# An S4 convolution beside multi-query attention: setup transfers, the order of the first arguments and keys, and SyncE in emission order

## The chip, the cores and the metric

The kernel runs on one core of a Trainium2 chip. The metric is the device time of one execution in microseconds (us). The engines are TensorE (PE), VectorE (DVE), ScalarE (ACT), GpSimd (POOL) and SyncE (SP, which only issues transfers).

## The reference

Two independent blocks on sequences of 2048 positions, their outputs side by side. All is float32.

```python
# block A: a diagonal state-space model, 576 channels, 128 states, as an FFT convolution
dt = exp(log_dt)[:, None]
logdA = dt * (A_re + 1j * A_im)
P = exp(logdA[:, :, None] * arange(2048))
K = einsum("dn,dnl,dn->dl", Cc, P, dt * Bc).real
y = irfft(rfft(pad(u)) * rfft(pad(K)))[:2048] + u * Dskip
# block B: attention with 32 heads of 18, one key and one value head for all
q = heads(x @ wq); k = x @ wk; v = x @ wv
p = softmax(einsum("bhqd,bkd->bhqk", q, k) * 18 ** -0.5)
b = merge(einsum("bhqk,bkd->bhqd", p, v)) @ wo
out = concatenate([y, b], axis=-1)
```

## The kernel before

The attention sets the pace. A main loop goes in steps of three exponentials: PE makes scores `s` (L493, 128 x 1024, in pairs of matmuls of `aug`, the queries, against `kaug`, the keys), ACT takes `P = exp(s)` (L502, L504), PE adds the products `ops` of `P` with the values (L802). There are 1024 such exponentials of 128 x 1024. The queries of a head are projected, split, and sent through DRAM (`qd`) into `aug` by loads on SP (L481, L482).

Between these, a planner puts the pieces of all other work: query and output projections and the convolution. It is run while the kernel is built. Each piece is a step of a generator (`Stream`), with a cost and a due time from a model of the engines (`Clock`); constants at the top (`RATE`, `PACE`, `LEAD`, `GAP` and more) say how early or late a piece may be taken. All this fill work writes one PSUM bank, so the next piece on PE waits until DVE has copied out the one before.

The convolution goes in 12 chunks of 48 channels. `front(k)` makes a chunk's kernel: `factors(k)` works out powers of the state matrix (`r`, `f`, `m`, `w`: arguments on DVE, exponentials and sines on ACT, then products on DVE), `tables` and `kgen` turn them into `kg` on PE, and DVE copies this into `ksb`. At the end, `ksb` is stored to DRAM as `kd` (L1187) and loaded again in another layout as `kt`, by four loads (L1189) that wait until `kd` has landed. `front(k + 1)` starts at once behind it, while `back(k)` transforms the inputs (`hu`, `lu` on PE, copied out to `scu` by DVE) and the kernel (`hk`, `lk`). Factors are made for two chunks at a time: an even chunk computes its own and those of the next, and stores the next chunk's as `park` in DRAM; the odd chunk loads them (`w`, `r`, `f`, `m`, L1075) and goes on with the products `r<-r,m` and `f<-f,m` on DVE.

The order of the instructions on PE, ACT and DVE is the order in which the program emits them. On SP (and POOL) a scheduler of the language sets it, by its own estimate of when each transfer can go.

In the setup, `x0`, `wq`, `wkv`, `xr` are loaded; PE projects the first queries (`qps`, `qc`, `rows`), then keys and values (`kps`, `kv`) of all 2048 positions, chunk by chunk of the 576 inputs (`project`). `kc` is a copy of the keys, `keys` their rounded form and its remainder, and `place_keys` sends both into `kaug`, the placed keys. `conv.begin(n)` lets the convolution emit its next steps at that point.

Of the kernel before, what the change touches and what calls it, by code (L numbers as in the profile page):

```python
# [9 lines left out]
F32 = mybir.dt.float32  # L10
F32R = mybir.dt.float32r
I32 = mybir.dt.int32
AF = mybir.ActivationFunctionType
# [4 lines left out]
P = 128  # L18
# [3 lines left out]
DH = 18  # L22
# [15 lines left out]
NP = 8  # L38


RATE = 3.7138
PACE = 3.4622
AHEAD = 0.5907
TOTAL = 375.4872
LAST = 732.5081
DEFER = 0.3214
NAUG = 5
LEFT = 2.4801
CAP = 1.4415
DEBT = 0.4509  # L50
GROUP = 0.1798
HOLD = 0.2063
LEAD = 1.4122
MOST = 0.6584
LEAST = 0.4776
NEAR = 0.65
SLOPE = 0.6122
SOON = 1.3784
URGENT = 9.2035
BACK = 2  # L60
HELD = 0
GAP = 0.2804
GAP_NEW = 0.4872

LATE = {1: [0], 3: [1], 5: [2], 6: [3]}

# [138 lines left out]
class Attention:  # L205
# [36 lines left out]
    def setup(self, tp, conv):  # L242
# [22 lines left out]
        self.x0 = x0 = self.xp.tile([P, 5, CT], F32, name="x0", tag="x")  # L265

        conv.early()
        for k in range(5):
            if k % 2 == 0:
                e = min(k + 2, 5)  # L270
                nc.sync.dma_start(self.wq[0][:, k:e, :], a["wq"][0, :, k:e, :])
            nc.sync.dma_start(x0[:, k, :], a["xT"][0, :, k, :] if k < 4 else a["xe"][0])
        nc.sync.dma_start(wkv, a["wkv"])
        nc.scalar.dma_start(place, a["place"])
        for k in range(4):
            nc.sync.dma_start(xr[:, k], a["xT"][1:4, :, k, :].rearrange("c p n -> p c n"))
            if k == 1:
                nc.sync.dma_start(xe, a["xe"][1])
        nc.scalar.dma_start(spread, a["spread"])
# [33 lines left out]
        conv.begin(9)  # L313
        nc.scalar.activation(qc[:mn, :], qps[:mn, :], AF.Copy)
        for j in range(2):
            matmul4(nc, rows[:, j, :], place[:mn, 1 + j, :], qc[:mn, :])
        for j in range(2):
            nc.scalar.activation(self.ring[j], rows[:, j, :], AF.Copy)
        conv.begin(1)
        ab = self.p2.tile([P, 3], F32, tag="ab", name="ab0_0")  # L320
        V.tensor_reduce(ab[:mn, 0:1], qc[:mn, :], axis=AX.X, op=ALU.max, apply_absolute_value=True)
        conv.begin(6)
        for j in range(2):
            put(self.ring[j], rows[:, j, :], 1 + j)
# [4 lines left out]
        nc.scalar.activation(self.kc, kps, AF.Copy)  # L329
        project(pv, 32, 3)  # L330
        matmul4(nc, kq[:, 1, :], place[:, 0, :], self.kc)
        V.tensor_reduce(km[:, 4:5], self.kc, axis=AX.X, op=ALU.max, apply_absolute_value=True)
        V.tensor_scalar(km[:, 0:4], spread[:, FLAG:FLAG + 4], km[:, 4:5], None, op0=ALU.mult)
        pk = self.bank(4, "kmx")
        nc.tensor.matmul(pk, spread[:, 0:P], km[:, 0:4], start=True, stop=True)
        nc.scalar.activation(keys[:, 0, :], self.kc, AF.Copy)
# [3 lines left out]
        put(self.kaug[:, 0:CT], kq[:, 1, :], 0)  # L340
        self.side_work = side = Stream(self.side(keys[:, 3, :], keys[:, 4, :], aw), self.k, 99.0)
        while self.queried == 0:
            side.advance()
        pk = self.ps_o.tile([P, CT], F32, tag="o", name="kmx4")[:, :16]
# [3 lines left out]
        nc.scalar.activation(self.vt, pv, AF.Copy)  # L348
        V.tensor_tensor(keys[:, 1, :], self.kc, keys[:, 0, :].bitcast(F32), op=ALU.subtract)
        for t, r in ((0, 0), (0, 36), (1, 18)):  # L350
            self.place_keys(keys[:, t, :], r)
# [13 lines left out]

    def values(self):
        nc, V, K = self.nc, self.V, self.k
        vp = self.bank(CT, "vp").rearrange("p (j n) -> p j n", j=4)
# [598 lines left out]
class Conv:  # L967
# [57 lines left out]
    def arguments(self, k, w, f, r, m):  # L1025

        nc, V, K = self.nc, self.V, self.k
        tt = V.tensor_tensor
        mu, ad, sb = ALU.mult, ALU.add, ALU.subtract
        raw = self.raw.pop(k)  # L1030
        dt = raw[:, 6, :]
        nc.scalar.activation(dt, dt, AF.Exp)
        yield "v", K.act(0.25) + 0.2, False
        tt(raw[:, 0:4, :], raw[:, 0:4, :], dt.unsqueeze(1).broadcast_to([P, 4, ND]), op=mu)
        av, bv, br, bi, cr, ci = (raw[:, j, :] for j in range(6))
        V.tensor_scalar(bv, bv, 1.0 / (2 * math.pi), None, op0=mu)
# [4 lines left out]
        tt(m, ch(av), row(1), op=mu)  # L1041
        yield "v", 0.0, False
        tt(w[:, 2, :], ci, bi, op=mu)
        tt(f, ch(bv), row(0), op=mu)
        if k < 2:
            nc.scalar.activation(m, m, AF.Exp)
        yield "v", 0.0, False
        tt(w[:, 1, :], cr, bi, op=mu)
        V.tensor_scalar(r, f, MAGIC, -MAGIC, op0=ad, op1=ad)
        yield "v", 0.0, False  # L1050
        tt(w[:, 0, :], w[:, 0, :], w[:, 2, :], op=sb)
        tt(f, f, r, op=sb)
        yield "v", 0.0, False
        tt(w[:, 2, :], ci, br, op=mu)
        V.tensor_scalar(r.bitcast(I32), f.bitcast(I32), 0x7FFFFFFF, None, op0=ALU.bitwise_and)
        yield "v", 0.0, False
        tt(w[:, 1, :], w[:, 1, :], w[:, 2, :], op=ad)
        if k > 1:
            self.load(k + 2)

    def factors(self, k):
# [10 lines left out]
        if k % 2:  # L1072
            n = ND * NF
            for j, t in enumerate((f, r, m, w)):
                nc.sync.dma_start(t, self.parked[:, j * n:min((j + 1) * n, 3 * n + 3 * ND)].rearrange("p (c n) -> p c n", n=t.shape[2]))  # L1075
            yield "v", K.t + 7.0, False
        else:
            two = p1.tile([P, 3 * ND * NF + 3 * ND], F32, tag="tab", name=f"two{k}")
            part = lambda j, n: two[:, j * ND * NF:j * ND * NF + n * ND].rearrange("p (c n) -> p c n", n=NF if n == NF else ND)
            f2, r2, m2, w2 = part(0, NF), part(1, NF), part(2, NF), part(3, 3)  # L1080
            yield from self.arguments(k, w, f, r, m)
            yield "v", 0.0, False
            yield from self.arguments(k + 1, w2, f2, r2, m2)
            yield "v", K.v + 0.3, False

            if k > 0:
                nc.scalar.activation(m, m, AF.Exp)
                nc.scalar.activation(m2, m2, AF.Exp)
            K.act(2.5)
            yield "b", K.v + 0.3, False  # L1090
            for a, b in ((r, f), (r2, f2)):
                nc.scalar.activation(a, a, AF.Sin, scale=-TWO_PI, bias=self.hp)
                nc.scalar.activation(b, b, AF.Sin, scale=TWO_PI)
            if k == 0:
                nc.scalar.activation(self.one, self.one, AF.Exp)
                for j in (2, 3):
                    self.load(j)
            self.parked = self.dr.tile([P, 3 * ND * NF + 3 * ND], F32, tag="park", name=f"park{k}")
            nc.sync.dma_start(self.parked, two)
            yield "v", K.act(7.7) + 0.3, False  # L1100
        tt(r, r, m, op=mu)
        yield "v", 0.0, False
        tt(f, f, m, op=mu)
# [208 lines left out]
    def early(self):  # L1312
        nc = self.nc
        nc.scalar.dma_start(self.con, self.a["con"])
        self.load(0, nc.scalar)
        self.load(1, nc.scalar)
        self.n = -1
        self.streams = [Stream(self.front(0), self.k)]

# [55 lines left out]
def build(tc, **aps):  # L1375
# [109 lines left out]
```

## Time and profile before

| | us |
|---|---|
| median of 3 runs | 1194.89 (1194.51 to 1195.13) |
| the profiled execution | 1192.97 |
| its span in the profile | 1191.2 |
| PE busy | 1137.7 |
| ACT busy | 1041.7 |
| DVE busy | 989.0 |
| POOL busy | 53.9 |
| first exponential of the loop starts at | 29.23 |

A row of the timeline has the start, the duration, the engine and its line, the operation with output and inputs, and in brackets the idle time of the engine ahead of it with what ended it. `SPq` and `POOLq` are the queues by which transfers are issued: their durations are those of issuing, not of the transfer. A row of the windows has the length, each engine's busy time, the clock granted to PE, the DMA engines' share and their GB/s. A row of the costliest groups has busy time and mean ns of one, then the engine's idle time ahead of them and what ended most of it.

### The profile page before, as it was taken

The numbers are of one execution on the slowest core, as the hardware profiler recorded it, in microseconds if no ns is written. First come the engines' busy times: TensorE is split into PE (matmuls) and PEld (weight loads), VectorE is DVE, ScalarE is ACT, GpSimd is POOL, SyncE is SP. The second block draws the span as 40 slices with busy tenths as digits, with TensorE's granted clock in tenths as the row PEclk, the third lists the DMA queues.
The fourth block names the chain that finished last, engine by engine and source line by source line (L and its number), as shares of the span: only waits on it lengthen the run. The fifth ranks groups of instructions, "written<-read, shape, count | busy, mean of one in ns | idle before, by whom it ended". The sixth has DMA issues, their size and how long they took to land.

```text
span 1191.2 us, 41260 instructions
## 1 busy us (share of the span) xinstructions
PE 1137.7 (96%) x17954; PEld 599.6 (50%) x17954; DVE 989.0 (83%) x1733; ACT 1041.7 (87%) x1095; POOL 53.9 (5%) x104
## 2 busy tenths in 40 slices
PE   8999999899999999999989999999999989999997
PEld 2455455455555455555535545544544545544543
DVE  6859969986996985996997798598799797799576
ACT  5889899989898988889888988999998998998993
POOL 1100100111000000010000000001000000000000
PEclk9899999999999999999989999999999999999999
DMA  8541232424123123122233401223401221410201
GB/s 296 174 148 52 97 128 62 150 90 170 58 84 106 66 90 130 59 99 91 72 124 116 143 28 36 88 71 111 138 31 55 98 114 53 148 47 21 76 29 57
DMA packets 50185, 113.34 MB, mean 95 GB/s; under 512 B 6964, under 2 KB 17300, under 8 KB 48719
## 3 DMA queue, kind: packets, MB, share of 16 engines
q1 hardware_dynamic: 43919, 95.88, 23.2%
q0 software_dynamic: 5360, 14.03, 3.3%
q8 instruction: 143, 2.34, 0.8%
q10 hardware_dynamic: 720, 0.73, 0.2%
q14 instruction: 43, 0.35, 0.1%
HBM read 61.51 MB, written 48.45 MB: 92 GB/s over the span
## 4 chain that ended last, share of the span: by engine, by line
PE 53%; DVE 36%; ACT 4%; DMA 3%; issue 3%; SPq 1%; DVEq 0%; ACTq 0%
PE ops L802 21%; PE s L493 15%; DVE tab L128 7%; DVE acc L128 5%; DVE ks L128 4%; PE op L202 3%; PE iy L202 3%; ACT P L504 3%; DVE pt L128 2%; PE kg L1168 2%; PE q L202 2%; DVE tt L128 2%; DVE two L128 1%; DVE sck L128 1%; PE lu L202 1%
## 5 line engine op out<-in xcount | busy, mean ns | idle before, releaser
L504 ACT ACTIVATE P<-s 128x1024 f32<-128x1024 f32 x992 | 943.4, 1032 | 111.3 <-PE s L493 102.3
L802 PE MATMUL ops<-P,v_sb 128*32 128x256 f32 x8192 | 540.0, 382 | 6.3 <-DVE o L132 6.1
L493 PE MATMUL s<-aug,kaug 55*128 55x512 f32 x2048 | 351.6, 439 | 8.3 <-ACT P L504 7.2
L802 PEld LDWEIGHTS ops<-P,v_sb 128*32 128x32 f32 x8192 | 242.3, 110 | 191.6 <-issue 58.3
L493 PEld LDWEIGHTS s<-aug,kaug 55*128 55x128 f32 x2048 | 167.5, 185 | 203.6 <-ACT P L504 108.3
L202 PE MATMUL op<-wo_sb,oT 126*32 126x288 f32 (+1 forms) x1144 | 84.1, 410 | 7.2 <-DVE ob L132 6.3
L202 PE MATMUL q<-x,wq_sb 128*32 128x256 f32 x1200 | 78.7, 392 | 4.5 <-DVE un L140 2.2
L132 DVE COPY ksb<-kg 128x192 f32<-128x192 f32 x48 | 17.3, 361 | 67.0 <-PE kg L1168 66.9
L128 DVE TENSOR_TENSOR tab<-tab,tt 128x576 f32<-128x576 f32 (+1 forms) x72 | 59.0, 820 | 1.3
L128 DVE TENSOR_TENSOR tab<-sum,r 128x576 f32<-128x576 f32 (+1 forms) x72 | 58.8, 816 | 0.0
L128 DVE TENSOR_TENSOR tab<-r,dif 128x576 f32<-128x576 f32 (+1 forms) x72 | 58.7, 815 | 0.0
L128 DVE TENSOR_TENSOR tab<-tab 128x576 f32<-128x576 f32 (+1 forms) x72 | 58.6, 814 | 0.0
L128 DVE TENSOR_TENSOR tt<-f,sum 128x576 f32<-128x576 f32 (+1 forms) x72 | 58.6, 814 | 0.0
L202 PEld LDWEIGHTS q<-x,wq_sb 128*32 128x32 f32 x1200 | 37.0, 112 | 37.7 <-issue 9.4
L128 DVE TENSOR_TENSOR acc<-acc,pt 128x864 f32<-128x864 f32 (+2 forms) x72 | 54.3, 754 | 1.4
L128 DVE TENSOR_TENSOR pt<-us,ks 128x864 f32<-128x864 f32 (+2 forms) x72 | 54.2, 753 | 1.3
L202 PEld LDWEIGHTS op<-wo_sb,oT 126*32 126x32 f32 (+1 forms) x1144 | 32.1, 109 | 44.6 <-issue 9.6
L128 DVE TENSOR_TENSOR u<-u,iy 128x384 f32<-128x384 f32 x24 | 13.3, 553 | 38.3 <-PE iy L202 38.1
L1168 PEld LDWEIGHTS kg<-tab 128*32 128x32 f32 x2304 | 37.1, 110 | 15.0 <-issue 5.8
L1168 PE MATMUL kg<-tab 128*32 128x64 f32 x2304 | 41.5, 220 | 3.0 <-DVE tab L128 2.5
L128 DVE TENSOR_TENSOR ks<-ks 128x576 f32<-128x576 f32 (+1 forms) x48 | 41.0, 853 | 0.7
L202 PE MATMUL iy<-w,dft_sb 128*32 128x192 f32 x768 | 37.6, 328 | 3.5 <-DVE ql L128 2.6
(160 smaller groups left out, 996.9 us busy)
## 6 DMA issues: line engine op xcount, KB each, us to landing
aug<-qd SPq DMA_DIRECT2D x124, 108.0 KB
park<-two SPq DMA_DIRECT2D x6, 1944.0 KB
od<-o SPq DMA_DIRECT2D x31, 256.0 KB
qd<-qh POOLq DMA_DIRECT2D x30, 256.0 KB, 2.9
u<-u SPq DMA_DIRECT2D x12, 480.0 KB
kd<-ksb SPq DMA_DIRECT2D x12, 384.0 KB
kt<-kd SPq DMA_DIRECT2D x48, 96.0 KB
outa<-u SPq DMA_DIRECT2D x12, 384.0 KB
```

The costliest lines, as they stand in the source:

```text
L128: return self.v.tensor_tensor(out, a, b, **k)
L132: return self.v.tensor_copy(out, src)
L202: nc.tensor.matmul(ps[j:e], w[:, j:e], x, start=start, stop=stop, tile_position=(0, j))
L493: nc.tensor.matmul(ps[:, j, :], self.kaug[r, kb * P:(kb + 1) * P], t[r, :], start=True, stop=True)
L504: nc.scalar.activation(pt, ps, AF.Exp, scale=SCALE)
L802: nc.tensor.matmul(o_ps[32 * j:32 * j + 32, cs], self.v[:, kb, :], pts[2 * n + j // 2][:, j % 2, cs], start=(kb + f == 0), stop=(kb + f == ...
L1168: nc.tensor.matmul(ps[32 * g:32 * g + 32, d, :], t[:, :32], t[:, 32:], start=(j == 0), stop=(j == 1), tile_position=(0, 32 * g))
```

## The change

- The first transfers: `wq` of the first query group in two pieces instead of three, `x0` in two pieces of two and one of one instead of five; `place` goes by SP instead of ACT, `spread` and the second `raw` by POOL.
- In the setup the first chunks' arguments are emitted in another order, and a chunk's sines as soon as its arguments are there; `put` of the first queries comes earlier.
- Keys are projected ahead of three of the five value projections; the copies `kc`, `keys` and `vt` are made by DVE instead of ACT; two value projections come later, one of them after the first scores.
- `place_keys` stores a part of the keys to DRAM (`kr`) and loads it into `kaug` with three transfers per part and queue pair, where 18 transfers went from SBUF to SBUF.
- SP is taken into the engines whose order is that of emission.
- All constants of the planner have new values.

```diff
-RATE = 3.7138
-PACE = 3.4622
+RATE = 6.5889
+PACE = 3.8504
...
-        for k in range(5):
-            if k % 2 == 0:
-                e = min(k + 2, 5)
-                nc.sync.dma_start(self.wq[0][:, k:e, :], a["wq"][0, :, k:e, :])
-            nc.sync.dma_start(x0[:, k, :], a["xT"][0, :, k, :] if k < 4 else a["xe"][0])
+        for k, e in ((0, 2), (2, 4)):
+            w = slice(k, e if k == 0 else 5)
+            nc.sync.dma_start(self.wq[0][:, w, :], a["wq"][0, :, w, :])
+            nc.sync.dma_start(x0[:, k:e, :], a["xT"][0, :, k:e, :])
+        nc.sync.dma_start(x0[:, 4, :], a["xe"][0])
         nc.sync.dma_start(wkv, a["wkv"])
-        nc.scalar.dma_start(place, a["place"])
+        nc.sync.dma_start(place, a["place"])
...
-        for k in (0, 1, 4, 2):
+        for k in (0, 1):
             project(kps, 0, k)
             project(pv, 32, k)
-        project(kps, 0, 3)
-        nc.scalar.activation(self.kc, kps, AF.Copy)
-        project(pv, 32, 3)
-        matmul4(nc, kq[:, 1, :], place[:, 0, :], self.kc)
+        for k in (4, 2, 3):
+            project(kps, 0, k)
+        project(pv, 32, 4)
+        V.tensor_copy(kc, kps)
+        matmul4(nc, kq[:, 1, :], place[:, 0, :], kc)
...
-    def place_keys(self, t, r):
-
-        for c in range(1, NCH):
-            for b in (0, 64):
-                (self.nc.sync if b else self.nc.gpsimd).dma_start(self.kaug[b + r:b + r + 18, c * CT:(c + 1) * CT].bitcast(F32), t[32 * c:32 * c + 18, :].bitcast(F32))
+    def place_keys(self, n, t, *rows):
+
+        kd = self.dr.tile([P, CT], F32, tag="kr", name=f"kr{n}", bufs=2)
+        self.nc.sync.dma_start(kd, t.bitcast(F32))
+        kd = kd.rearrange("(c d) n -> d c n", c=4)[:DH, 1:]
+        for r in rows:
+            for b, q in ((0, self.nc.sync), (64, self.nc.gpsimd)):
+                q.dma_start(self.kaug[b + r:b + r + DH, CT:].bitcast(F32).rearrange("d (c n) -> d c n", c=3), kd)
...
+            def sines(cos, sin):
+                nc.scalar.activation(sin, sin, AF.Sin, scale=TWO_PI)
+                nc.scalar.activation(cos, cos, AF.Sin, scale=-TWO_PI, bias=self.hp)
+            one, two_ = self.arguments(k, w, f, r, m), self.arguments(k + 1, w2, f2, r2, m2)
+            if k == 0:
+                take = lambda g, n: [next(g, None) for _ in range(n)]
+                take(one, 2)
+                take(two_, 1)
+                take(one, 1)
+                take(two_, 1)
+                yield "v", 0.0, False
+                take(one, 9)
+                sines(r, f)
+                yield "v", 0.0, False
...
-        with tc.manual_schedule(engines={mybir.EngineType.PE, mybir.EngineType.Activation, mybir.EngineType.DVE}):
+        with tc.manual_schedule(engines={mybir.EngineType.PE, mybir.EngineType.Activation, mybir.EngineType.DVE, mybir.EngineType.SP}):
```

Where the chunks 0 and 1 meet, SP's order was this (`od0` is the attention's output of a first pair of heads, `aug2` the next queries; the numbers behind the names tell tiles of one name apart):

```order
L513 DMA od0_362<-o0_0_955 128x512
L1075 DMA r1_1150<-park0_250 128x1248
L1075 DMA f1_1149<-park0_250 128x1248
L1075 DMA m1_1151<-park0_250 128x1248
L1187 DMA kd0_1140<-ksb0_511 128x768
L1189 DMA kt0_1139<-kd0_1140 32x4x192 x4
L481 DMA aug2_113<-qd0_309 54x1x512
L482 DMA aug2_113<-sd0_310 1x512
```

And now, at the same place on SP:

```order
L522 DMA od0_340<-o0_0_944 128x512
L1213 DMA kd0_1187<-ksb0_500 128x768
L1215 DMA kt0_1186<-kd0_1187 32x4x192 x4
L1084 DMA f1_1196<-park0_380 128x1248
L1084 DMA r1_1197<-park0_380 128x1248
L1084 DMA m1_1198<-park0_380 128x1248
L1084 DMA w1_1195<-park0_380 128x144
L490 DMA aug2_113<-qd0_296 54x1x512
```

The reloads of chunk 1's parked factors have moved from ahead of the store `kd` to behind the four loads `kt` (`w1`, which stood further ahead, too). It is the same for the chunks 3, 5, 7, 9 and 11.

In the setup, PE's order from the last groups of key and value projections to the placing of the keys (`kq<-kc`) was this:

```order
L307 MATMUL kps<-x_130,wkv_sb 32x512
L307 MATMUL kps<-xr,wkv_sb 32x512 x3
L307 MATMUL kv<-x_130,wkv_sb 32x512
L307 MATMUL kv<-xr,wkv_sb 32x512 x3
L307 MATMUL kps<-x_130,wkv_sb 32x512
L307 MATMUL kps<-xr,wkv_sb 32x512 x3
L307 MATMUL kv<-x_130,wkv_sb 32x512
L307 MATMUL kv<-xr,wkv_sb 32x512 x3
L202 MATMUL kq<-kc,place_sb 32x512 x4
L335 MATMUL kmx<-km,spread_sb 128x4
```

And now:

```order
L307 MATMUL kps<-x_130,wkv_sb 32x512
L307 MATMUL kps<-xr,wkv_sb 32x512 x3
L307 MATMUL kps<-x_130,wkv_sb 32x512
L307 MATMUL kps<-xr,wkv_sb 32x512 x3
L307 MATMUL kv<-x_130,wkv_sb 32x512
L307 MATMUL kv<-xe,wkv_sb 32x512
L307 MATMUL kv<-x_130,wkv_sb 32x512
L307 MATMUL kv<-xe,wkv_sb 32x512
L202 MATMUL kq<-kc,place_sb 32x512 x4
L338 MATMUL kmx<-km,spread_sb 128x4
L307 MATMUL kv<-x_130,wkv_sb 32x512
L307 MATMUL kv<-xr,wkv_sb 32x512 x3
```

The key projections now end one value projection (that of `xe`) ahead of `kq<-kc`; the value projections of two input chunks have moved behind it.

More of the change, by code (lines that the diff above doesn't have):

```diff
@@ L38 @@
 NP = 8
-RATE = 3.7138
-PACE = 3.4622
[L43 to L46, printed above, removed]
-NAUG = 5
[L48 to L59, printed above, removed]
+RATE = 6.5889
+PACE = 3.8504
+AHEAD = 0.6137
+TOTAL = 321.2393
+LAST = 905.5416
+DEFER = 0.3529
+NAUG = 5
+LEFT = 2.4147
+CAP = 1.5789
+DEBT = 0.543
+GROUP = 0.214
+HOLD = 0.2599
+LEAD = 0.995
+MOST = 0.9497
+LEAST = 0.6398
+NEAR = 1.0011
+SLOPE = 0.7522
+SOON = 1.2746
+URGENT = 7.8913
 BACK = 2
 HELD = 0
-GAP = 0.2804
-GAP_NEW = 0.4872
+GAP = 0.2104
+GAP_NEW = 0.4801
 LATE = {1: [0], 3: [1], 5: [2], 6: [3]}
@@ L319, in setup @@
         conv.begin(1)
+        put(self.ring[0], rows[:, 0, :], 1)
+        conv.begin(1)
+        put(self.ring[1], rows[:, 1, :], 2)
         ab = self.p2.tile([P, 3], F32, tag="ab", name="ab0_0")
         V.tensor_reduce(ab[:mn, 0:1], qc[:mn, :], axis=AX.X, op=ALU.max, apply_absolute_value=True)
-        conv.begin(6)
-        for j in range(2):
-            put(self.ring[j], rows[:, j, :], 1 + j)
-        for k in (0, 1, 4, 2):
+        for k in (0, 1):
             project(kps, 0, k)
             project(pv, 32, k)
-        project(kps, 0, 3)
-        nc.scalar.activation(self.kc, kps, AF.Copy)
-        project(pv, 32, 3)
-        matmul4(nc, kq[:, 1, :], place[:, 0, :], self.kc)
-        V.tensor_reduce(km[:, 4:5], self.kc, axis=AX.X, op=ALU.max, apply_absolute_value=True)
+        for k in (4, 2, 3):
[3 more added lines that the diff above has]
+        matmul4(nc, kq[:, 1, :], place[:, 0, :], kc)
+        V.tensor_reduce(km[:, 4:5], kc, axis=AX.X, op=ALU.max, apply_absolute_value=True)
         V.tensor_scalar(km[:, 0:4], spread[:, FLAG:FLAG + 4], km[:, 4:5], None, op0=ALU.mult)
+        V.tensor_copy(keys[:, 0, :], kc)
         pk = self.bank(4, "kmx")
         nc.tensor.matmul(pk, spread[:, 0:P], km[:, 0:4], start=True, stop=True)
-        nc.scalar.activation(keys[:, 0, :], self.kc, AF.Copy)
         nc.scalar.activation(self.kaug[:, 0:CT], kq[:, 1, :], AF.Identity, bias=spread[:, FLAG + 6:FLAG + 7])
@@ L343, in setup @@
             side.advance()
+        self.place_keys(0, keys[:, 0, :], 0, 36)
+        self.last = lambda: project(pv, 32, 3)
         pk = self.ps_o.tile([P, CT], F32, tag="o", name="kmx4")[:, :16]
@@ L347, in setup @@
         V.tensor_reduce(self.kmax[:, 1:5], pk.rearrange("p (m c) -> p m c", c=4), axis=AX.X, op=ALU.max)
[L348 to L351, printed above, removed]
-    def place_keys(self, t, r):
-        for c in range(1, NCH):
-            for b in (0, 64):
-                (self.nc.sync if b else self.nc.gpsimd).dma_start(self.kaug[b + r:b + r + 18, c * CT:(c + 1) * CT].bitcast(F32), t[32 * c:32 * c + 18, :].bitcast(F32))
+        V.tensor_tensor(keys[:, 1, :], kc, keys[:, 0, :].bitcast(F32), op=ALU.subtract)
+        self.place_keys(1, keys[:, 1, :], 18)
+        self.pv = pv
+    def place_keys(self, n, t, *rows):
[5 more added lines that the diff above has]
+                q.dma_start(self.kaug[b + r:b + r + DH, CT:].bitcast(F32).rearrange("d (c n) -> d c n", c=3), kd)
     def late_setup(self):
@@ L367, in values @@
         nc, V, K = self.nc, self.V, self.k
+        self.last()
+        V.tensor_copy(self.vt, self.pv)
         vp = self.bank(CT, "vp").rearrange("p (j n) -> p j n", j=4)
@@ L1041, in arguments @@
         tt(m, ch(av), row(1), op=mu)
+        if k < 2:
+            nc.scalar.activation(m, m, AF.Exp)
         yield "v", 0.0, False
@@ L1080, in factors @@
             f2, r2, m2, w2 = part(0, NF), part(1, NF), part(2, NF), part(3, 3)
[L1081 to L1086, printed above, removed]
+            def sines(cos, sin):
[12 more added lines that the diff above has]
+                yield "v", 0.0, False
+                take(two_, 3)
+                yield "v", 0.0, False
+                take(two_, 9)
+                sines(r2, f2)
+                nc.scalar.activation(self.one, self.one, AF.Exp)
+                yield "v", 0.0, False
+                for j in (2, 3):
+                    self.load(j)
+            else:
+                yield from one
+                yield "v", 0.0, False
+                yield from two_
+                yield "v", K.v + 0.3, False
                 nc.scalar.activation(m, m, AF.Exp)
                 nc.scalar.activation(m2, m2, AF.Exp)
[L1089 to L1097, printed above, removed]
+                K.act(2.5)
+                yield "b", K.v + 0.3, False
+                sines(r, f)
+                sines(r2, f2)
             self.parked = self.dr.tile([P, 3 * ND * NF + 3 * ND], F32, tag="park", name=f"park{k}")
             nc.sync.dma_start(self.parked, two)
-            yield "v", K.act(7.7) + 0.3, False
+            yield "v", K.act(7.7 if k > 0 else 0.0) + 0.3, False
         tt(r, r, m, op=mu)
@@ L1315, in early @@
         self.load(0, nc.scalar)
-        self.load(1, nc.scalar)
+        self.load(1, nc.gpsimd)
         self.n = -1
```

8 lines of the change are left out of this document (4 added, 4 removed).

## The prediction

> **What bounds the kernel now.** I read the page first (busy times, the chain that ended last), then the waits of PE and ACT, then the timeline of the setup, and last the timeline of the stretches in which a chunk of the convolution is handed over to the next one.
>
> ```profile
> PE 1137.7 (96%) x17954; PEld 599.6 (50%) x17954; DVE 989.0 (83%) x1733; ACT 1041.7 (87%) x1095; POOL 53.9 (5%) x104
> ...
> PE 53%; DVE 36%; ACT 4%; DMA 3%; issue 3%; SPq 1%; DVEq 0%; ACTq 0%
> ...
> L504 ACT ACTIVATE P<-s 128x1024 f32<-128x1024 f32 x992 | 943.4, 1032 | 111.3 <-PE s L493 102.3
> ```
>
> PE is busy for 1137.7 of 1191.2 us, and ACT's idle time ahead of the exponentials is put down to PE's scores. So nearly every microsecond for which PE stands still is a microsecond of the run. DVE has room (83%) but carries 36% of the chain: PE waits for it through the single bank in which all fill work lands. Two places are moved by the change: the setup, up to the first exponential at 29.23, and the six hand-overs from an even chunk to an odd one, at 75 to 96 and five times more.
>
> **The setup.**
>
> ```profile
> PE kq L202 <- DMA x<-xT: 1.8, 3, 0.9
> ```
> ```profile
> 21.20 0.60 PE L307 MATMUL kps<-xr,wkv_sb 128*32 128x512 f32 x3
> ...
> 22.92 0.61 PE L307 MATMUL kps<-xr,wkv_sb 128*32 128x512 f32 x3
> ...
> 23.77 1.03 PE L307 MATMUL kv<-xr,wkv_sb 128*32 128x512 f32 x6
> ```
> ```profile
> 24.77 0.20 ACT L1095 ACTIVATE one_sb<-one_sb 128x1 f32<-128x1 f32 x1
> 24.88 0.58 ACT L329 ACTIVATE kc<-kps 128x512 f32<-128x512 f32 x1
> ...
> 29.23 6.14 ACT L502 ACTIVATE P<-s,nb 128x1024 f32<-128x1024 f32 x6 [1.41 <-PE s L493]
> 37.96 3.12 ACT L502 ACTIVATE P<-s,nb 128x1024 f32<-128x1024 f32 x3 [2.59 <-PE s L493]
> ```
> ```profile
> 31.00:37.00 6.00, 5.58 (x46) 2.35 (x44) 3.54 (x4) 4.37 (x5) 0.36 (x1) 0.50 0.57 171
> ```
>
> Before, the last key projection (22.92) ends at about 23.8, but its copy `kc` starts only at 24.88, when ACT has ended its sines, a table load and the small exponential at 24.77. From the copy's end (25.46) to the first exponential at 29.23 it takes 3.77.
>
> The change puts the copy on DVE, which lies idle by then, and moves the key projections ahead of two value projections: two groups of (22.92 - 21.20) / 2 = 0.86 each, 1.7 earlier. Two value projections then follow between the copy and the first scores or just behind them, in PE's idle time there. The first transfers' waits on x were 1.8 in all; with three fewer of them in front I count that as gained for the query projection. Against this, ACT now runs an exponential of chunk 1 ahead of the copy `qc`, so the placed rows and all projections behind them start later than they could, by one or two of its instructions. The last key projection then ends at about 22.0, the copy at 22.5, and the first exponential is at 22.5 + 3.77 = 26.3 instead of 29.23: **3.0 gained**. The ends: 0 when ACT's later sines and table loads still end at 24.97 and the keys' bias waits for them, 5.5 when the projections follow the transfers with no wait at all.
>
> From 31 to 37 PE was granted half its clock, and ACT stood 2.59 idle at 37.96 for it. With less idle time in PE ahead of this, the stretch may go; it may as well only shift. Between 0 and 2.6 I take 1.0.
>
> The keys' placement by way of DRAM adds a store and one landing to what the scores against the later keys need.
>
> ```profile
> 32.41 0.80 PE L493 MATMUL s<-aug,kaug 55*128 55x512 f32 x2 [0.21 <-DMA kaug<-keys]
> ```
>
> Before, one pair of scores waited 0.21 for it. Afterwards the keys' second part is worked out on DVE at about 26, and its store goes out then; by the time from `kd` to `kt` below (2.64 to 3.14), and as much again for the load, it lands at 31 to 33. The first scores that read other keys than the first quarter stand, now as before, behind the query projection that comes ahead of the exponentials at 37.96; some 4 us earlier they are due at about 34. Price 0 to 2; I take 0 and keep the 2 for the range. Setup in all: 4.0 gained.
>
> **The hand-over of parked factors.** This is the larger term. An even chunk works out the factors of itself and of the next one; the next one's `f`, `r`, `m` lie parked in DRAM. SyncE has one queue and waits in its order. Before, the scheduler had put the three reloads ahead of the store `kd` and the four loads `kt`:
>
> ```profile
> 75.84 0.34 SPq L1075 DMA_DIRECT2D r<-park  x1
> 76.51 0.95 SPq L1075 DMA_DIRECT2D f<-park  x1
> 77.51 0.42 SPq L1075 DMA_DIRECT2D m<-park  x1
> 83.70 0.32 SPq L1187 DMA_DIRECT2D kd<-ksb  x1
> 86.84 1.76 SPq L1189 DMA_DIRECT2D kt<-kd  x4
> ```
> ```profile
> 90.28 1.45 DVE L128 TENSOR_TENSOR r<-r,m 128x1248 f32<-128x1248 f32 x1
> 91.64 1.45 DVE L128 TENSOR_TENSOR f<-f,m 128x1248 f32<-128x1248 f32 x1
> 93.01 0.55 DVE L132 COPY scu<-hu 128x384 f32<-128x384 f32 x1
> ```
> ```profile
> 94.44 0.86 PE L202 MATMUL lu<-u,dft_sb 128*32 128x192 f32 x16
> ```
>
> In emission order SyncE comes to `kd`, then to `kt`, which waits until `kd` has landed, and only then to `f`, `r`, `m`. The product `r<-r,m` stands on DVE where it stood, 6.58 behind the issue of `kd`; behind it on DVE stands the copy `scu<-hu` that clears PE's bank for `lu`. That copy ends at 93.56, PE reaches `lu` at 94.44: 0.9 of slack. The sixth hand-over has the same 6.56, and the fourth 5.28:
>
> ```profile
> 1029.19 0.32 SPq L1187 DMA_DIRECT2D kd<-ksb  x1
> ```
> ```profile
> 1035.75 1.45 DVE L128 TENSOR_TENSOR r<-r,m 128x1248 f32<-128x1248 f32 x1
> ```
> ```profile
> 663.73 0.34 SPq L1075 DMA_DIRECT2D r<-park  x1
> ...
> 670.20 0.32 SPq L1187 DMA_DIRECT2D kd<-ksb  x1
> 672.84 1.75 SPq L1189 DMA_DIRECT2D kt<-kd  x4
> ```
> ```profile
> 675.48 1.45 DVE L128 TENSOR_TENSOR r<-r,m 128x1248 f32<-128x1248 f32 x1
> ```
> ```profile
> 669.00:670.00 1.00, 1.00 (x54) 0.88 (x48) 0.19 (x1) 0.60 (x1) 0.00 (x0) 1.00 1.06 424
> 670.00:671.00 1.00, 1.00 (x14) 0.47 (x14) 0.17 (x1) 0.72 (x1) 0.00 (x0) 1.00 0.12 45
> ```
>
> The steps behind `kd`: 2.64 (672.84 - 670.20) to 3.14 (86.84 - 83.70) until `kt` is issued, 1.75 for its four issues, so `f` goes out at 4.4 to 4.9. From the first of the three issues to the last byte it took about 6.3 (663.73 to 670.0, where the rate falls from 424 to 45 GB/s). So `m` is there at 10.7 to 11.2 behind `kd`; I take 11.0. DVE stands for 11.0 - 6.6 = 4.4 in four hand-overs and for 11.0 - 5.28 = 5.7 in two (the rows of the second and third read like the first, of the fifth like the fourth). PE loses that less its slack of 0.9: 4 x 3.5 + 2 x 4.8 = **23.6**.
>
> The Trainium skill (DMA: Bandwidth & Descriptors, section Specifications) gives an HBM limit of about 358 GB/s for one core. The row at 669 shows 424, so here the measurement decides; by the page's figure the 1.9 MB would land an estimated 0.9 later and the six stalls would be some 5 us more.
>
> The kernel before has had one such stall, in the third hand-over, where the scheduler had put `m` behind `kd`:
>
> ```profile
> 479.58 1.46 DVE L128 TENSOR_TENSOR r<-r,m 128x1248 f32<-128x1248 f32 x1 [2.34 <-DMA m<-park]
> ```
> ```profile
> 483.48 1.50 PE L202 MATMUL q<-x,wq_sb 128*32 128x256 f32 x24 [1.44 <-DVE scu L128]
> ```
> ```profile
> 486.38 2.86 ACT L504 ACTIVATE P<-s 128x1024 f32<-128x1024 f32 x3 [1.84 <-PE s L493]
> ```
>
> DVE's 2.34 became 1.44 on PE (again 0.9 of slack) and 1.84 on ACT: the wait does reach the exponentials. This 1.4 is paid already, so the six add **22.2**.
>
> A long pause can also cost clock. The one long pause of PE in the loop before:
>
> ```profile
> 606.40 0.27 PE L202 MATMUL up<-aw,all 128*32 128x8 f32 x13 [3.62 <-DVE aw L136]
> ```
> ```profile
> 612.81 2.85 ACT L504 ACTIVATE P<-s 128x1024 f32<-128x1024 f32 x3 [3.00 <-PE s L493]
> ```
> ```profile
> 607.00:614.00 7.00, 5.65 (x50) 2.24 (x46) 6.90 (x13) 4.00 (x5) 0.52 (x1) 0.52 0.88 348
> ```
>
> After it the clock was half for some 6.5 us, and ACT missed 3.00. There PE had a second pause close by, so 3.62 alone may not do it. Ends: 0, and all six for 18; I take one, of the two pauses of 4.8, for **3.0**. The Trainium skill (TensorE: Matmul & The Clock Gate, on the clock gate) has the clock halved when PE idles over a free-running window of about 3.4 us; by that the four pauses of 3.5 would hardly ever trip it and each of 4.8 in an estimated four cases of ten, 2 to 3 us in all.
>
> **What costs nothing.** The `aug` loads stand behind `kd` and `kt` now as before; the three issues more ahead of them take about 1.7 (75.84 to 77.51), and the stalls push their scores back by more. The planner's constants change the order only finely: PE's work per step keeps its sum and the chunks stand at the same steps. With no row for them, I put 0, and 3 to either side.
>
> **Sum.** The profiled execution took 1192.97: 1193.0 - 4.0 + 22.2 + 3.0 = 1214.2. The median of the three runs shown lies 1.9 above it (1194.89): **1216.1**. A measurement of this kernel can tell about 0.2% from no change, 2.4 us.
>
> **Rivals.** First, the stalls don't reach PE, and the setup alone counts: 1194.9 - 4.0 = **1190.9**, faster. For it `m` must be there within 7.5 (6.6 + 0.9) behind `kd`, or PE must come to `lu` by one of its steps (about 3.1, three exponentials of 1.03) later than before, as a planner with other constants can bring about; from 3.5 of such delay on the four shorter stalls vanish. For: the constants are all new. Against: 7.5 is earlier than the sum of `kt`'s wait and the loads' own 6.3, whatever else is moved, and in the order the same rows stand between the last `kg` and `lu`. I give it 0.2. Second, the half clock comes with every stall: 5 x 3.0 more, **1231**; 0.08. Third, stalls of a microsecond or less, which give the setup's gain back: within 0.2%; 0.04. The forecast has the remaining 0.68, with a range of its own of 1206 to 1227 (setup 0 to -7, landing 1 either way for six stalls, one trip more or less).
>
> **Range and chances.** The forecast's own range leaves out too much, since the faster case has 0.2: I reach down to 1188 and up to 1229. Faster 0.2, within 0.2% 0.04, slower 0.76.
>
> **What would show it.** Right: on SyncE's timeline `f`, `r`, `m` behind `kt`, their issue 4 to 5 behind `kd`; on DVE `r<-r,m` with 4 to 6 of idle time released by the DMA `m<-park`, six times; on PE `lu` with 3 to 5 released by DVE `scu`; the first exponential at about 26. Wrong: no PE wait at `lu` although `m` is late (then PE's order has more in front of it); `f`, `r`, `m` landing within 8 of `kd`; or another wait, of the exponentials above all, that is new and larger than these.

## The result: 1265.41 us, slower by 6 per cent, and the profile after

| | before | after |
|---|---|---|
| median | 1194.97 (4 runs) | 1265.41 (4 runs, 1261.79 to 1270.14) |
| ratio | | 1.0597 [1.0571, 1.0624] |
| span of the profiled execution | 1191.2 | 1262.3 |
| mean granted clock | 0.993 | 0.967 |
| first exponential | 29.23 | 25.79 |

One of the five executions of `b_emit` (below), the profiled one, took 1575.35 at a granted clock of 0.65; that kernel is judged by the other four.

The page of the kernel after (busy times; the chain that ended last; the exponentials with the idle time ahead of them; the two groups at the hand-over):

```profile
PE 1157.4 (92%) x17954; PEld 610.3 (48%) x17954; DVE 994.8 (79%) x1737; ACT 1039.7 (82%) x1092; POOL 52.7 (4%) x100
...
PE 51%; DVE 31%; DMA 10%; issue 3%; SPq 2%; ACT 2%; POOL 0%; DVEq 0%; ACTq 0%; POOLq 0%
...
L513 ACT ACTIVATE P<-s 128x1024 f32<-128x1024 f32 x992 | 942.6, 1030 | 178.4 <-PE s L502 168.9
...
L202 PE MATMUL lu<-u,dft_sb 128*32 128x192 f32 x384 | 24.4, 380 | 34.7 <-DVE scu L132 34.7
...
L128 DVE TENSOR_TENSOR r<-r,m 128x1248 f32<-128x1248 f32 x12 | 17.5, 1455 | 39.7 <-DMA m<-park 39.7
```

DMA is now 10% of the chain, it was 3%. The work hardly changed (PE is 20 us busier for the same 17954 matmuls, at a mean clock of 0.967 instead of 0.993); ACT's wait for scores grew from 102.3 to 168.9. Two rows name the foreseen stall: DVE waits 39.7 for `m<-park`, PE 34.7 behind it at `lu`.

The first hand-over on SyncE's queue, DVE and PE, then the exponentials:

```profile
93.54 0.33 SPq L1213 DMA_DIRECT2D kd<-ksb  x1
96.83 1.75 SPq L1215 DMA_DIRECT2D kt<-kd  x4
98.62 0.43 SPq L1084 DMA_DIRECT2D f<-park  x1
99.09 0.43 SPq L1084 DMA_DIRECT2D r<-park  x1
99.57 0.43 SPq L1084 DMA_DIRECT2D m<-park  x1
```
```profile
107.42 1.46 DVE L128 TENSOR_TENSOR r<-r,m 128x1248 f32<-128x1248 f32 x1 [7.22 <-DMA m<-park]
```
```profile
110.76 1.51 PE L202 MATMUL lu<-u,dft_sb 128*32 128x192 f32 x16 [6.35 <-DVE scu L132]
```
```profile
115.66 2.86 ACT L513 ACTIVATE P<-s 128x1024 f32<-128x1024 f32 x3 [8.86 <-PE s L502]
```

`f` goes out 5.1 behind `kd`, near the 4.4 to 4.9 worked out, but the product that waits for `m` starts only 13.9 behind it (11.8 to 14.3 in the six hand-overs), not 11.0. PE pauses 6.35, and ACT stands idle for 8.86, 2.5 more than the pause. Over the end of the pause and the work behind it the granted clock (third from the right) is 0.56:

```profile
107.00:118.00 11.00, 7.24 (x74) 3.53 (x78) 10.34 (x17) 2.34 (x3) 0.00 (x0) 0.56 0.08 29
```

A stall that wasn't foreseen stands where the attention's outputs of a quarter of the queries are scaled (`normalize`: `od` to DRAM, its sums `dn` back, their reciprocals `rden` to DRAM, spread over the heads as `db`):

```profile
651.95 0.34 SPq L522 DMA_DIRECT2D od<-o  x1
657.60 0.58 SPq L535 DMA_DIRECT2D dn<-od  x1
658.27 0.62 SPq L1335 DMA_DIRECT2D outa<-u  x1
660.98 0.33 SPq L1030 DMA_DIRECT2D u<-u  x1
661.41 0.38 SPq L539 DMA_DIRECT2D rden<-dn  x1
661.85 3.85 SPq L542 DMA_DIRECT2D oT<-od  x5
```
```profile
659.83 0.23 DVE L136 TENSOR_SCALAR dn<-dn 128x128 f32<-128x128 f32 x1 [5.50 <-DMA dn<-od]
...
674.45 0.69 DVE L128 TENSOR_TENSOR oT<-oT,db 126x512 f32<-126x512 f32 x1 [4.74 <-DMA db<-rden]
```
```profile
669.18 2.85 ACT L513 ACTIVATE P<-s 128x1024 f32<-128x1024 f32 x3 [7.21 <-PE s L502]
...
684.06 2.85 ACT L513 ACTIVATE P<-s 128x1024 f32<-128x1024 f32 x3 [5.31 <-PE s L502]
```

Behind these two waits of DVE for a transfer, ACT stands idle for 7.21 and 5.31 in one chunk of queries. On SyncE the chain shares the queue with the `aug` loads ahead of `od`, with the convolution's `outa` and `u`, and with its own five `oT` loads. The reciprocals are done at 661.04 and `rden` goes out at 661.41, but `db` only at 665.74, behind the five loads. In the kernel before, the scheduler had issued these loads one by one, from 480 on for the chain at 624, and `db` went out 1.7 behind `rden`:

```profile
480.15 2.57 SPq L533 DMA_DIRECT2D oT<-od  x2
...
542.81 0.81 SPq L533 DMA_DIRECT2D oT<-od  x1
...
576.81 0.80 SPq L533 DMA_DIRECT2D oT<-od  x1
...
623.68 0.59 SPq L526 DMA_DIRECT2D dn<-od  x1
624.32 0.67 SPq L533 DMA_DIRECT2D oT<-od  x1
628.91 0.33 SPq L530 DMA_DIRECT2D rden<-dn  x1
```

The start of the n-th of the 1024 exponentials, as a difference to before (from ACT's timeline of the profiled execution of each kernel; a minus is earlier; the kernels are those of the experiments):

```
n                    0    32    64    80   400   528   544   912  1008
after             -3.4   4.6   3.7  12.4  21.8  27.1  38.9  71.0  71.2
a_early           -3.3   3.9   3.4   2.8   7.1   5.2  16.9  30.5  30.8
a_early_pool      -3.2   4.7   3.7   3.2   9.3   8.7  13.5  22.1  22.6
a_sched           -2.9   5.4   4.5   3.9   6.1   4.2   4.1   9.3   9.6
a_direct          -3.2  -3.7  -4.2  -4.8  -1.1  -2.8  -3.2   5.1   5.2
b_const           -1.1  -1.7  -2.3  -2.8  -1.4  -3.4  -3.7   5.1   5.1
```

The first row shows three losses: 8 in the first 32 exponentials, steps of 5 to 9 at the six hand-overs (the first between 64 and 80), and one of 12 between 528 and 544.

### The profile page after: what moved, and what is told of

It reads as the page before. It is cut to its first block, busy times and chain, and to the rows that moved or that the text cites. A ratio compares the mean times of both kernels' runs of the same rounds, so it can differ in the third digit from the quotient of the medians.

```text
span 1262.3 us, 41206 instructions
## 1 busy us (share of the span) xinstructions
PE 1157.4 (92%) x17954; PEld 610.3 (48%) x17954; DVE 994.8 (79%) x1737; ACT 1039.7 (82%) x1092; POOL 52.7 (4%) x100
## 4 chain that ended last, share of the span: by engine, by line
PE 51%; DVE 31%; DMA 10%; issue 3%; SPq 2%; ACT 2%; POOL 0%; DVEq 0%; ACTq 0%; POOLq 0%
PE ops L811 20%; PE s L502 14%; DVE tab L128 7%; DVE acc L128 4%; DVE ks L128 4%; PE op L202 3%; DMA m<-park 3%; PE iy L202 2%; PE kg L1194 2%; PE q L202 2%; DVE pt L128 2%; DVE tt L128 2%; DVE two L128 2%; PE lu L202 1%; DMA db<-rden 1%
## 5 line engine op out<-in xcount | busy, mean ns | idle before, releaser
L513 ACT ACTIVATE P<-s 128x1024 f32<-128x1024 f32 x992 | 942.6, 1030 | 178.4 <-PE s L502 168.9
L811 PEld LDWEIGHTS ops<-P,v_sb 128*32 128x32 f32 x8192 | 250.2, 111 | 191.3 <-issue 52.4
L202 PE MATMUL op<-wo_sb,oT 126*32 126x288 f32 (+1 forms) x1152 | 86.8, 422 | 8.2 <-DVE ob L132 4.1
L202 PE MATMUL lu<-u,dft_sb 128*32 128x192 f32 x384 | 24.4, 380 | 34.7 <-DVE scu L132 34.7
L128 DVE TENSOR_TENSOR r<-r,m 128x1248 f32<-128x1248 f32 x12 | 17.5, 1455 | 39.7 <-DMA m<-park 39.7
```

The costliest lines, as they stand in the source:

```text
L128: return self.v.tensor_tensor(out, a, b, **k)
L202: nc.tensor.matmul(ps[j:e], w[:, j:e], x, start=start, stop=stop, tile_position=(0, j))
L513: nc.scalar.activation(pt, ps, AF.Exp, scale=SCALE)
L811: nc.tensor.matmul(o_ps[32 * j:32 * j + 32, cs], self.v[:, kb, :], pts[2 * n + j // 2][:, j % 2, cs], start=(kb + f == 0), stop=(kb + f == ...
```

## The experiments

**Undoing SyncE's order (a_sched).**

```diff
-EngineType.PE, EngineType.Activation, EngineType.DVE, EngineType.SP
+EngineType.PE, EngineType.Activation, EngineType.DVE
```

> The changed kernel with SyncE's order left to the scheduler again; all else (setup, planner's constants) as changed. If SyncE's emission order is what costs the time, the six waits of r<-r,m for m<-park go, no half clock follows them, and the time is 1187 to 1194 (1194.9 less the setup's 3.4 measured at the first exponential, constants within 3). If the planner's new constants cost a part of it, the time stays above 1205, with PE's waits spread over the loop. If the setup's new transfers cost it, above 1205 with a late start.

1204.92, ratio to before 1.0094 [1.006, 1.0127]. Of the 70.4 lost, 60.5 are SyncE's order: the waits for `m` and for `db` are gone, that for `dn` is 1.2, and ACT's wait for scores is 106.1, near the 102.3 of before. But it isn't 1187 to 1194: some 11 are left. Between the first and the 32nd exponential the kernel goes from 2.9 ahead to 5.4 behind, and it loses 5 more near the end (the table, 544 to 912). In the first stretch there stands this, on PE:

```profile
40.14 1.32 PE L502 MATMUL s<-aug,kaug 55*128 55x512 f32 x2 [5.82 <-DMA kaug<-kr]
```

**The order alone, on the kernel before (b_emit).**

```diff
-EngineType.PE, EngineType.Activation, EngineType.DVE
+EngineType.PE, EngineType.Activation, EngineType.DVE, EngineType.SP
```

> The kernel before, with SyncE in emission order and nothing else changed. If the order is the whole cost: 1194.9 plus about 70 (the 73 lost in the loop after the first exponential, and the setup's transfers as before), so 1255 to 1275, with six waits of DVE for m<-park of 6 to 7 each. If the constants carry half of it: 1220 to 1240.

1281.71, ratio 1.0723 [1.0693, 1.0753], more than the 1255 to 1275 expected: 87.7 for the order alone, where it cost the changed kernel 60.5. So the order has no one price. Why it is 27 more here stays open, and whether DVE waits for `m` here as expected isn't shown.

**The reloads ahead of the store (a_early).**

```diff
             yield from self.tables(k, s)
+            if s == NSB - 1 and k % 2 == 0:
+                self.preload(k + 1)      # the loads of f, r, m, w
             yield from self.kgen(k, s, ksb)
...
-        if k % 2:
-            for j, t in enumerate((f, r, m, w)):
-                nc.sync.dma_start(t, ...)
+        w, f, r, m = self.reload if k % 2 else self.factor_tiles(k)
```

> The changed kernel, SyncE still in emission order, but the even chunk emits the next chunk's four reloads (f, r, m, w) after its last table, ahead of its last kgen, the store kd and the loads kt. If the reloads alone cost the time at the hand-overs: the six jumps of 5 to 9 against before (46 together) go, less the one stall that before had, and 1265.4 becomes 1215 to 1226; what is left are the waits for dn and db of the attention's scaling. If the order's other waits are what matters: above 1240.

1229.39 (1224.98 to 1236.42), 36.0 less. All waits for `m<-park` are gone, and so are the steps at the hand-overs (2.8 at the 80th exponential, not 12.4); the 5.0 that it still loses at the sixth, between the 896th and the 912th, is 4.5 in `b_const` (below), which has no wait for `m` either. 3 more than expected is left, and the waits of the scaling are now the largest of DVE's for a transfer, 22.8 where the changed kernel had 15.0:

```profile
DVE oT L128 <- DMA db<-rden: 14.8, 5, 4.9
DVE dn L136 <- DMA dn<-od: 8.0, 2, 5.6
```

**The setup alone (b_setup):** the changed kernel with SyncE's order by the scheduler and the planner's constants of before.

```diff
-RATE = 6.5889
+RATE = 3.7138
...
-GAP_NEW = 0.4801
+GAP_NEW = 0.4872
```

> The changed kernel with the planner's constants of before and SyncE's order left to the scheduler: the setup's change alone. By the first exponential, 3.4 earlier in the changed kernel: 1191 to 1192.5. If the time gained is lost again in the first heads (the changed kernel had given back 1.8 and 1.5 within its first four steps): 1194 to 1196.

1281.81, ratio 1.0716 [1.0675, 1.0758]: neither expectation. The first exponential is at 26.3, the convolution then slips: in the emitted order the last chunk's `kg` stands at the steps 329 to 341 of 341, before at 312 to 323, and its transforms are left for the end, where PE waits 23.1 in one piece for DVE and ACT 48.9 for the last product. With the old constants the new setup makes the planner order the work otherwise, so this run doesn't price the setup; `a_direct` and `b_const` do, with the new constants.

**A pause of known length (b_delay).**

```diff
         tt(f, f, m, op=mu)
+        for _ in range((k + 1) // 2 if k % 2 else 0):
+            nc.vector.tensor_tensor(m, m, m, op=mu)
```

> The kernel before with 1, 2, 3, 4, 5 and 6 more products m*m (on a tile that is no longer read, 1.37 each) on DVE behind f<-f,m in the first to sixth hand-over, unknown to the planner: pauses of known length at the place where the changed kernel waits. PE's slack there was 0.9, so PE should pause for 0.5, 1.8, 3.2, 4.6, 6.0 and 7.3 (the third is 1 to 2 longer, since m is late there anyway). If a long pause also costs half the clock: no lower clock after the first two, 0.50 for some 6 us after the last three, and the exponentials lose the pause plus about 3. If it is the pause alone: each loss equals its pause, 23 in sum, and the clock rows stay at 1.00.

1226.2 in one run. The fourth pause, on DVE, PE and ACT, and the clock:

```profile
686.65 5.94 DVE L1105 TENSOR_TENSOR m<-m 128x1248 f32<-128x1248 f32 x4
```
```profile
693.11 1.51 PE L202 MATMUL lu<-u,dft_sb 128*32 128x192 f32 x16 [5.08 <-DVE scu L132]
```
```profile
697.65 5.81 ACT L504 ACTIVATE P<-s 128x1024 f32<-128x1024 f32 x6 [7.20 <-PE s L493]
```
```profile
692.00:696.00 4.00, 2.89 (x32) 1.58 (x36) 4.00 (x9) 0.00 (x0) 0.00 (x0) 0.50 0.18 70
```

PE paused 0.61, 2.07, 5.15, 5.08, 6.50 and 8.00. Around the first two the clock stayed at 1.00; during the other four it fell, and PE went on at 0.50. The exponentials were set back by 0.7, 3.0, 6.3, 6.5, 7.7 and 10.1 against before (the third had a pause of 1.44 in before). Beyond the pause (less that 1.44) this is 0.1 and 0.9 where the clock stayed, and 2.6, 1.4, 1.2 and 2.1 where it fell. So the pause itself is most of the price, and a trip to half the clock adds no more than 1.2 to 2.6, not 3.0. The Trainium skill (TensorE: Matmul & The Clock Gate, on the clock gate) puts the idle window at about 3.4 us. The trace agrees with that length, but not with idleness as the condition: in the fourth hand-over the clock fell at 690.05, behind 3.41 us in which PE was busy for 1.39 (the last section has more).

**The constants alone (b_const).**

```diff
-RATE = 3.7138
+RATE = 6.5889
...
-GAP_NEW = 0.4872
+GAP_NEW = 0.4801
```

> The kernel before with the planner's constants of the changed one, nothing else. The prediction put 0 and 3 to either side: 1192 to 1198. The setup with the old constants went to 1281.8, so the constants and the setup may belong together: then this one is slower than 1200 too. If the new constants alone are better, below 1191.

1199.94, ratio 1.005 [1.0033, 1.0068]: 5.9 slower, beyond the prediction's 3. In the profiled execution it is 1 to 4 ahead for most of the loop and loses 9 near the end (the table, 544 to 912); for what, was not followed.

**The keys' way (a_direct):** `a_sched` with the keys placed from SBUF to SBUF.

```diff
-        self.nc.sync.dma_start(kd, t.bitcast(F32))
...
-            for b, q in ((0, self.nc.sync), (64, self.nc.gpsimd)):
-                q.dma_start(self.kaug[b + r:b + r + DH, CT:]..., kd)
+            for c in range(1, NCH):
+                for b in (0, 64):
+                    (self.nc.sync if b else self.nc.gpsimd).dma_start(self.kaug[b + r:b + r + DH, c * CT:(c + 1) * CT], t[32 * c:32 * c + DH, :])
```

> The changed kernel with SyncE's order left to the scheduler (1204.9) and the keys placed from SBUF to SBUF, by 18 transfers as before, instead of through DRAM. If the wait of the scores for kaug<-kr (5.8 on PE, 7.2 on ACT at 43 us) is the price of the way through DRAM: 1195 to 1199, and the exponentials at step 10 are 5 to 8 earlier than in that run. If the first steps lose the time to something else (the value projections, the half clock): 1203 to 1206.

1196.98 (1195.09 to 1200.78), 7.9 less. At the 32nd exponential it is 9 ahead of `a_sched`, which had waited for the keys there; at the 1008th it is still 4.4 ahead in the two profiled executions, and 7.9 by the medians of all. With the scheduler's order, the way through DRAM cost that. Against `b_const`, which differs by the setup (and the order of two sines), it is 3.0 ahead by the medians (ratios to before 1.0021 [1.0006, 1.0036] and 1.005 [1.0033, 1.0068]): that is what the rest of the setup's change is worth, though the two profiled executions end level (5.2 and 5.1).

**Three tries on the scaling's chain**, all on top of `a_early`. First (a_early_norm) the five `oT` loads right behind `dn`:

```diff
         nc.sync.dma_start(dn[:n, :], od[h0:h1, DH, :]...)
+        for m in ms:
+            nc.sync.dma_start(o[:mn, m, :], od[...])
         yield "v", K.t + 6.0, False
...
-        for m in ms:
-            nc.sync.dma_start(o[:mn, m, :], od[...])
```

> The changed kernel with the early reloads (1229.4), and in the attention's scaling the five loads oT<-od emitted right behind dn<-od, not between rden<-dn and db<-rden. If those loads ahead of db are what made DVE wait for db<-rden (14.8 in five) and the clock fall behind it: the jump of 12 at step 178 and those of 4 to 5 at steps 94 and 301 shrink to a third, 1208 to 1218. If the scaling's waits come from the store od and dn<-od alone: no more than 3 gained, 1226 to 1230.

1234.26 (1227.4 to 1234.63): nothing gained. The wait for `db` is still there, for another reason:

```profile
646.45 0.41 SPq L1345 DMA_DIRECT2D outa<-u  x1
654.31 0.34 SPq L1030 DMA_DIRECT2D u<-u  x1
654.75 0.38 SPq L542 DMA_DIRECT2D rden<-dn  x1
```

`u<-u` waits until the store `outa` has landed, and `rden`, whose reciprocals were done at 645.39, stands behind it for 9.4. Second (a_early_od), the stores `od` by GpSimd:

```diff
-        nc.sync.dma_start(self.od[c][g * P:(g + 1) * P, :], o_sb)
+        nc.gpsimd.dma_start(self.od[c][g * P:(g + 1) * P, :], o_sb)
```

> The changed kernel with early reloads (1229.4) and the stores od<-o issued by GpSimd, so that they no longer stand behind the aug loads in SyncE's order. If the late od (4 behind its copy) is what makes dn late (DVE 8.0 in two): dn's waits fall below 3 and the jump of 12 at step 178 to 6 or less, 1215 to 1224. If db behind the other transfers decides: no more than 3 gained.

1229.56: the wait for `dn` fell from 8.0 to 3.8, that for `db` grew from 14.8 to 17.6, the time stayed. Third (a_early_pool), the whole chain by GpSimd, so that it has a queue without the convolution's transfers (`nc.sync` becomes `nc.gpsimd` for `od`, `dn`, `rden`, `oT`, `db`):

> The same with all transfers of the attention's scaling (od, dn, rden, oT, db) on GpSimd's queue. If what is left of SyncE's order after the early reloads (24.5 against the run with the scheduler, 1204.9) is that chain: 1205 to 1212. If it is spread over the other transfers (u, outa, outb, park, aug): above 1218.

1214.13 (1211.87 to 1216.06), 15.3 less than `a_early` and between the two cases expected. The wait for `db` is down to this:

```profile
DVE oT L128 <- DMA db<-rden: 0.6, 1, 0.6
```

That is most of what SyncE's order still cost (24.5), where neither of the single steps had gained anything. Whether `rden`, `oT` and `db` alone would have done it was not run; the wait for `dn` is still 6.7. Some 9 remain between it and `a_sched`. DVE waits 5.0 for `park` and 3.6 for `outb` here, neither of which it does in `a_sched`; what these waits cost was not separated.

**Versions that may beat both.** The reloads' early place on the kernel before, where one hand-over had a late `m` (b_early, the edit of `a_early` on the kernel before):

> The kernel before (SyncE's order by the scheduler) with the four reloads emitted by the even chunk ahead of its last kgen. Only the third hand-over had a late m there (DVE 2.34, PE 1.44). If such a wait costs what PE loses: 1.0 to 2.0 faster, 1192 to 1193.5, and no wait of r<-r,m. If the reloads' place is worth nothing where a scheduler sets the order: the same within 0.5.

1192.30 against 1194.01, ratio 0.9987 [0.9977, 0.9997]: 1.7 faster, where 1.0 to 2.0 was expected from PE's wait of 1.44. It is the one version here that beats the kernel before, by 0.1 per cent. And with the part of the setup that leaves the planner's steps alone (b_best):

```diff
-        for k in (0, 1, 4, 2):
-            project(kps, 0, k)
-            project(pv, 32, k)
-        project(kps, 0, 3)
-        nc.scalar.activation(self.kc, kps, AF.Copy)
-        project(pv, 32, 3)
+        for k in (0, 1):
+            project(kps, 0, k)
+            project(pv, 32, k)
+        for k in (4, 2, 3):
+            project(kps, 0, k)
+        project(pv, 32, 4)
+        nc.vector.tensor_copy(self.kc, kps)
...
+        project(pv, 32, 2)        # ahead of the first scores
+        self.last = lambda: project(pv, 32, 3)   # behind them
```

> The same, and of the setup only what kept its order of the convolution's steps: the larger first transfers, the key projections ahead of the value projections, and the copies kc, keys and vt on DVE; keys placed from SBUF to SBUF, old constants, so that the main loop's order is that of before. If the setup's gain is real where the planner's steps are left alone: the first exponential at 26.3 to 27.5 and 1189 to 1191.5. If the first exponentials' gain is lost in the first steps (a value projection behind the first scores, the half clock): 1192 to 1194.

1193.55, ratio 0.9999 [0.9988, 1.001]: no gain. The first exponential comes 2.7 earlier, then

```profile
26.52 3.13 ACT L507 ACTIVATE P<-s,nb 128x1024 f32<-128x1024 f32 x3 [1.38 <-PE s L498]
32.99 3.13 ACT L507 ACTIVATE P<-s,nb 128x1024 f32<-128x1024 f32 x3 [3.35 <-PE s L498]
```
```profile
28.00:31.00 3.00, 2.30 (x10) 0.20 (x8) 0.63 (x1) 1.65 (x2) 1.00 (x2) 0.50 0.65 199
```

the value projection that now stands behind the first scores runs at half the clock, and 1.7 of the 2.7 are given back within 16 exponentials.

## Why the prediction was right and wrong, step by step

**The hand-overs: right in kind, too small.** All six stalls came, on the engines and lines named: DVE 39.7 where 29.0 was worked out (4 x 4.4 + 2 x 5.7), PE 34.7 where 23.6 was. The term that was mis-sized is the landing: 6.3 from the first issue to the last byte, read from the rate of the windows. The product itself started 8.8 behind the first issue (107.42 - 98.62; 7.2 to 8.8 in the six). Here too the rate fell about 6.4 behind the first issue (383 GB/s from 104 to 105, 131 from 105 to 106), but DVE went on some 2 later. The rate shows when bytes stop, not when the waiting engine may go on; and in the row the 6.3 came from, `r<-r,m` was never waited for, so the row could not show it.

**The half clock: right in kind, too few.** One trip was taken; the clock fell at each of the six (0.56 over 107 to 118 for the first), as the second rival had it. By `b_delay` each adds at most 1.2 to 2.6, less than that rival's 3.0. Together with the pauses `a_early` puts the reloads at 36.0, where 25.2 was worked out (22.2 and 3.0). The 36.0 are a net figure: without the pauses, DVE's waits for `dn` and `db` grew from 15.0 to 22.8.

**What failed: "What costs nothing".** SyncE's order was followed at the one place where a large transfer changed sides. Under this head the prediction names the `aug` loads, rightly (PE has no wait for them in the changed kernel), and the constants. The scaling's chain is not mentioned, so its price stood at nothing without a row. In one queue the slack isn't each chain's own: in the changed kernel `db` stood behind the five `oT`, in `a_early_norm` `rden` stood behind `u`, which waited for `outa`. By `a_sched` the order costs 60.5, 24.5 beyond the reloads, 15.3 of it this chain. The measured time lies 49.3 above the forecast; these 24.5 are half of that, 10.8 are the reloads, 7.9 the keys, 5.9 the constants.

**The keys through DRAM: the wait was within the range given, the price with the other order was not.** 0 to 2 was given. In the changed kernel PE waited 1.11 for `kaug<-kr`; but the store of `park` went out at 39.26, behind the keys' transfers and others, and DVE waited 5.22 for it until 46.89. With the scheduler's order the way through DRAM cost 7.9 (`a_sched` against `a_direct`): there the 1.9 MB of `park` went out at 22.88, ahead of the two small stores, and PE waited 5.82 for the keys. What the way costs in emission order was not run.

**The setup: the first exponential was right, the gain was not.** 26.3 was worked out, 25.79 measured. The gain was then carried on to the end of the sum; in the changed kernel it was gone by the 32nd exponential. In that stretch lie the waits for the keys and for `park` and the half clock; their shares were not separated, but with the scheduler's order and the keys from SBUF to SBUF (`a_direct`) the kernel was still 3.7 ahead there. The half clock from 31 to 37 did not go, it moved to 28 to 35.

**The constants:** 0 and 3 to either side; 5.9 slower on the kernel before (`b_const`).

Put together from the runs: before 1194.0; the constants +5.9; the setup less the keys' way -3.0; the keys' way +7.9; the reloads +36.0; the scaling's chain +15.3; the rest of SyncE's order +9.2: 1265.3. The sum closes of itself, since each part is the difference of one kernel's median to the next; and as the executions of one kernel lie up to 11 apart (`a_early`), a part is good to some microseconds only. The parts belong to this one order of undoing; `b_emit` and `b_setup` show that other orders give other sizes.

## What to carry to other kernels

When a queue is taken from a scheduler into emission order, go through every transfer on it that waits for another transfer's landing, and write down what stands behind it: the slack of the chains in one queue is shared. Here moving one transfer of a chain to another queue gained nothing, moving all of them 15.3. A time at which data land is read from an instruction that waited for them, not from the rate. A gain in a setup is counted where the loop has taken it up, here some tens of exponentials later.

## What the runs showed of the hardware that was not expected

PE's clock fell to half at every pause of 4.25 to 8.00 of these two kernels (four in `b_delay`; in the changed kernel the six hand-overs with 4.25 to 6.66, and one of 4.67 in the scaling), and at neither of the hand-overs of `b_delay` with 0.61 and 2.07. But the length of the pause alone doesn't decide. In the changed kernel one of 2.00 that ended at 54.69 was followed by half the clock, one of 2.98 that ended at 241.07 was not.

What the traces show is a grid: in each of them all changes of the granted clock in the loop lie whole multiples of 3.41 us apart, and PE's busy time in the stretch of the grid that has just ended goes with whether the clock falls. The first stretch below holds the pause of 2.00, with PE busy for 1.41; the pause of 2.98 lies across the two others, with 1.87 and 1.98:

```profile
51.91:55.32 3.41, 1.41 (x18) 0.72 (x22) 3.31 (x8) 2.99 (x3) 0.00 (x0) 1.00 0.18 70
55.32:58.73 3.41, 3.41 (x36) 1.46 (x26) 3.38 (x6) 0.14 (x1) 0.54 (x1) 0.50 0.15 41
...
236.22:239.64 3.42, 1.87 (x28) 0.68 (x25) 3.35 (x7) 3.41 (x4) 0.00 (x0) 1.00 0.00 0
239.64:243.05 3.41, 1.98 (x39) 1.44 (x40) 3.38 (x9) 3.39 (x3) 0.00 (x0) 1.00 0.17 73
243.05:246.46 3.41, 2.24 (x52) 1.73 (x48) 2.56 (x6) 3.08 (x4) 1.64 (x3) 1.00 1.04 429
```

Over the traces of before, after and the experiments other than `b_emit`, from 60 us on to the last exponential, the clock fell behind all 54 stretches at full clock in which PE was busy for less than 0.40 of the time, behind 34 of the 82 with 0.40 to 0.61, and behind none of the 4045 with more. In the setup it is otherwise: there the clock of the changed kernel fell at 28.01 behind a stretch with 0.71.

The price beyond the pause stayed between 1.2 and 2.6 in `b_delay`; at the six hand-overs of the changed kernel ACT stood idle 2.0 to 2.8 longer than PE.
